# A fused attention and mixture kernel on one core: a new order for its 2,644 steps

## The chip, the cores and the metric

One Trainium2 chip, one of its cores. The metric is the device time of one execution in microseconds (us); lower is better. TensorE is called PE here, VectorE DVE, ScalarE ACT, GpSimd POOL, and SyncE, which issues the DMAs, SP.

## The reference

Attention with a learned bias over positions, followed by a soft mixture of experts. Sizes: 8 batches, 8 heads, 576 positions, head size 64; 8 experts with 4 slots each, inner size 1024; all in float32.

```python
scores = q @ k.T / sqrt(D)
x = log1p(abs(i - j)) / log1p(max(i, 1))
h = maximum(x[..., None] @ w1 + b1, 0)
scores += (h @ w2).transpose(2, 0, 1)
attn = softmax(scores)
x = (attn @ v).reshape(8 * 576, 512)
logits = x @ phi
slot_input = softmax(logits, axis=0).T @ x
slot_out[e] = maximum(slot_input[e] @ moe_w1[e], 0) @ moe_w2[e]
return softmax(logits, axis=1) @ slot_out
```

## The kernel before

**Stages.** First the bias tables are made (36 jobs): for each job ACT or DVE writes four feature rows (steps `f`, lines 975 and 977), PE multiplies them with the bias weights (`B`, line 987), ACT or DVE copies the product out of PSUM (`E`, lines 997 and 995) and SP stores it to a table in DRAM, `bias_m` (`D`, line 1006). From there it is read back, slanted, into tiles `bm` and `br` (`b`, line 425), once for each pair of heads.

Then come 40 units of attention (a pair of heads of one batch; for the first pair each batch is two smaller units, so units 0 to 15 are pair 0 and units 16 to 39 are pairs 1 to 3). A unit has two to four tiles of 128 query rows, and every second one also a fifth, numbered 4, made of the last 64 rows of two units. Tile p of unit u goes through these steps: scores on PE (`S`), bias and row minimum on DVE (`t`, line 534, twice, one a head), exponential on ACT (`e`, line 542, twice), 1e-9 added to the row sums on DVE or POOL (`a`, line 549), reciprocal on DVE (`m`, line 553), scaling on POOL (`n`, line 436, twice), transposes on PE (`T`, and `R` for the last 64 columns, line 495), copies into `at` on ACT or DVE (`c`, `cR`, line 439). The products with v are three steps `M0`, `M1`, `M2` of a unit (PE, line 629), whose result `x` copies and `xs` stores. `lq` and `lv` load q, k and v of a unit (lines 413 and 418).

In the units of the last pair, 32 to 39, the mixture joins in: `fx` reads a batch's stored results back (line 654, tile `xo`), `K`, `KR` transpose them, `L` makes logits (line 709), `D`, `W`, `C`, `Z` the running softmax and slot sums. Expert weights (`w`, `r`, line 957 and, for two tiles, 955; 64 of them, 512 KB each) are fetched as buffers fall free. At the end come the experts (`F`, line 1074; `s`, line 1147), `k` (transposes of the combine weights, lines 1120 and 1123), `g` (line 1157) and the outputs: products `o` (line 1179) and `X`, copies `p`, stores `P` (line 1187).

**Two forms of a score tile.** Line 509: `S` of tiles 0 to 3 is made either as two products of 64 rows by 128 columns of the PE array (line 517), here called *halves*, or as four of 64 by 64 (line 523), called *quarters*. The trace shows 8 matmul records of a tile in halves and 16 in quarters, since float32 takes two passes. Fifth tiles are always in quarters. Products with v use 64 by 64, transposes 64 by 128.

**What sets the order.** A table, `ORDER` (lines 24 to 245): each entry names a step and its unit, then a `+` that selects the other engine for a copy (for `S`: quarters), then after `@` the PSUM banks (eight banks; a tile of two banks starts at 0, 2, 4 or 6). The steps are sorted by their place in it, with no scheduler behind it (lines 481 to 488 and 1220):

```python
        def run():
            given[:] = spots
            f(eng)

        prog.append((at, len(prog), run))
...
        for _, _, f in sorted(prog, key=lambda x: x[:2]):
            f()
```

Each engine, SP's DMA issues included, works through its own instructions in this order and waits where an input is not there or a buffer is not free.

Of the kernel before, what the change touches and what calls it, by code (L numbers as in the profile page):

```python
# [29 lines left out]
f21.3/-1+ E8/-1 E10/-1 f16.1/-1+ f18.2/-1+ D14/-1 D12/-1 E19/-1 f16.3/-1 f17.0/-1 f23.1/-1+ f21.1/-1  # L30
B21/-1@6 f22.1/-1 f22.0/-1 f16.0/-1 B16/-1@4 f18.1/-1 f18.0/-1 B18/-1@2 E21/-1 f20.2/-1 D13/-1 D8/-1
f23.2/-1 f23.0/-1 f23.3/-1 B23/-1@0 D10/-1 E16/-1 D21/-1 f22.2/-1+ f22.3/-1 B22/-1@6 f1.2/-1 f17.3/-1
f17.2/-1 f17.1/-1+ B17/-1@4 f1.1/-1 E18/-1+ f20.0/-1+ f20.1/-1+ f5.0/-1 f3.1/-1+ E23/-1+ f0.2/-1 D19/-1
E22/-1 b1/-1 D16/-1 B20/-1@2 E20/-1+ E17/-1 D18/-1 f3.0/-1 f3.3/-1+ f1.0/-1+ S1/0@6,0 f5.1/-1
D22/-1 D23/-1 t1.0/0 S1/1+@4,2 t1.0/1 f1.3/-1+ B1/-1@6 f0.3/-1 t1.1/0 f5.2/-1 f3.2/-1+ B3/-1@4
f0.1/-1 f5.3/-1+ e1.0/0 e1.1/0 t1.1/1 f2.0/-1 D17/-1 B5/-1@0 a1/0 m1/0 E5/-1+ f0.0/-1+
f4.2/-1 B0/-1@2 E0/-1+ E1/-1 f2.3/-1+ f2.1/-1 f4.0/-1 S2/0@6,0 E3/-1 f2.2/-1+ f4.1/-1 D20/-1
b2/-1 f4.3/-1 e1.1/1 t2.1/0 lq/2 t2.0/0 n1.0/0 n1.1/0 T1/0@4 c1/0 B2/-1@2 E2/-1
B4/-1@4 E4/-1+ e2.1/0 S2/1@0,2 lq/3 e2.0/0 a2/0+ m2/0 e1.0/1 n2.1/0 t2.0/1 t2.1/1
a1/1+ S1/2@6,4 t1.1/2 f7.3/-1+ e2.0/1 n2.0/0 D0/-1 e2.1/1 a2/1 f7.2/-1 t1.0/2 m2/1  # L40
T2/0@0 c2/0 S2/2@2,4 f7.0/-1 m1/1 t2.1/2 e1.0/2 f30.3/-1 f27.3/-1 R2/0@6 t2.0/2 cR2/0
D5/-1 f6.1/-1 f7.1/-1 M0/0@0 f6.2/-1+ M1/0 lq/4 n2.0/1 f26.3/-1+ M2/0 lv/2 x/0
xs/0 e1.1/2 D4/-1 f6.0/-1 n2.1/1 T2/1@4 c2/1 n1.0/1 n1.1/1 T1/1@6 f24.1/-1 c1/1
R2/1@2 e2.1/2 cR2/1+ f27.0/-1 D2/-1 f28.2/-1 B7/-1@0 E7/-1+ D7/-1 a1/2 m1/2 n1.0/2
n1.1/2 f26.0/-1 S1/3+@2,4 t1.1/3 t1.0/3 e2.0/2 a2/2 e1.1/3 m2/2 f31.1/-1 f32.2/-1 M0/1@6
M1/1 S2/3+@0,4 t2.0/3 t2.1/3 f28.0/-1+ f26.1/-1 f24.2/-1 e1.0/3 D3/-1 D1/-1 a1/3+ m1/3
M2/1 x/1 f6.3/-1+ f33.0/-1 f26.2/-1 T1/2@2 c1/2 n2.1/2 n2.0/2 R2/2@0 f27.2/-1 T2/2@6
B6/-1@4 f33.3/-1 cR2/2 c2/2 f30.1/-1 E6/-1 S1/4+@2,0 t1.1/4 t1.0/4 M0/2@6 M1/2 n1.1/3
n1.0/3 f27.1/-1+ S2/4+@4,0 f25.2/-1+ M2/2 f28.3/-1 lq/5 B26/-1@2 t2.0/4 x/2+ e2.1/3 f28.1/-1+
e2.0/3 e1.0/4 e1.1/4 a1/4 t2.1/4 e2.1/4 f24.0/-1 B27/-1@4 f24.3/-1 E27/-1 a2/3 f33.1/-1  # L50
f30.0/-1 lq/6 m2/3 n2.0/3 B24/-1@6 E24/-1 E26/-1+ n2.1/3 D6/-1 D26/-1 m1/4 B28/-1@0
E28/-1+ n1.0/4 e2.0/4 a2/4+ T1/3@4 R2/3@2 c1/3+ cR2/3 xs/1 T2/3@6 lv/4 f25.1/-1
m2/4 n2.0/4 S1/5@0,2 D28/-1 t1.0/5 t1.1/5 n1.1/4 c2/3 D27/-1 S2/5@4,6 t2.1/5 t2.0/5
f34.0/-1 f30.2/-1+ B30/-1@0 f31.0/-1+ f32.1/-1+ n2.1/4 E30/-1 T1/4@2 c1/4+ f25.0/-1 R2/4@6 cR2/4
T2/4@4 e2.0/5 c2/4 S1/6+@0,6 t1.1/6 lv/3 M0/3@2 f32.0/-1 M0/4@4 f31.2/-1 M1/3 M1/4
M2/3 f29.3/-1 f29.0/-1 xs/2 D30/-1 f32.3/-1 f29.1/-1+ t1.0/6 f34.2/-1 M2/4 x/4+ b0/-1
f35.1/-1 lq/7 e1.1/5 e1.0/5 a1/5+ m1/5 n1.0/5 D24/-1 S2/6+@6,0 t2.1/6 t2.0/6 f25.3/-1+
x/3 B25/-1@2 f31.3/-1+ f29.2/-1+ xs/3 f34.3/-1+ e2.1/5 a2/5 f35.0/-1 lq/8 lv/5 m2/5
n2.0/5 e1.0/6 f35.3/-1+ B29/-1@4 E25/-1+ E29/-1+ B31/-1@0 E31/-1 B32/-1@6 n2.1/5 T2/5@2 E32/-1+
e1.1/6 c2/5+ lv/6 n1.1/5 R2/5@4 D25/-1 cR2/5 T1/5@0 c1/5 D29/-1 D31/-1 a1/6+  # L60
f35.2/-1 S1/7@6,4 t1.1/7 D32/-1 t1.0/7 S0/8@2,0 t0.0/8 b3/-1 m1/6 n1.0/6 f34.1/-1+ B34/-1@4
E34/-1+ D34/-1 B35/-1@6 E35/-1+ D35/-1 e2.1/6 e2.0/6 a2/6+ f33.2/-1+ B33/-1@2 m2/6 n2.1/6
e1.0/7 e1.1/7 a1/7+ m1/7 t0.1/8 n1.0/7 E33/-1 e0.0/8 S2/7+@4,6 D33/-1 t2.0/7 e2.0/7
M0/5@2 M1/5 lq/9 t2.1/7 e2.1/7 a2/7+ xs/4 m2/7 n1.1/7 S3/8+@0,4 t3.0/8 n2.0/6
M2/5 x/5 lv/7 b4/-1 n1.1/6 t3.1/8 n2.1/7 T1/6@6 c1/6 n2.0/7 R2/6@0 cR2/6+
T1/7@2 c1/7 xs/5 R2/7@4 T2/7@0 cR2/7+ c2/7+ T2/6@6 c2/6 S0/9+@4,2 t0.0/9 t0.1/9
S4/8@0,6 e0.1/8 a0/8 M0/6@4 M0/7@2 M1/6 M1/7 lq/10 e3.1/8 e3.0/8 a3/8+ m3/8
n3.0/8 n3.1/8 M2/6 t4.0/8 e4.0/8 t4.1/8 e4.1/8 x/6+ xs/6 m0/8 M2/7 x/7+
a4/8 n0.0/8 e0.0/9 m4/8 n4.0/8 S3/9+@0,6 t3.1/9 e0.1/9 e3.1/9 t3.0/9 S0/10@4,2 t0.1/10
T3/8@6 c3/8 n0.1/8 t0.0/10 T0/8@0 c0/8 R3/8@2 cR3/8+ n4.1/8 R4/8@4 T4/8@6 c4/8  # L70
cR4/8+ a0/9 m0/9 n0.0/9 S3/10@2,4 t3.1/10 e3.0/9 lv/9 e0.1/10 e3.1/10 t3.0/10 a3/9+
m3/9 n0.1/9 lv/8 M0/8@0 lq/11 S4/10@6,4 t4.0/10 e4.0/10 n3.1/9 n3.0/9 t4.1/10 e4.1/10
a4/10 m4/10 n4.0/10 n4.1/10 M1/8 M2/8 x/8 R3/9@2 cR3/9 xs/7 T3/9@6 T0/9@4
c0/9 c3/9+ S0/11+@0,2 t0.0/11 e3.0/10 a3/10 e0.0/11 m3/10 n3.0/10 S3/11+@6,4 t3.0/11 t3.1/11
lq/12 M0/9@0 M1/9 w0/22 lv/10 t0.1/11 lq/13 n3.1/10 e0.0/10 a0/10+ m0/10 n0.0/10
b0/15 S0/12+@6,4 t0.0/12 e3.0/11 M2/9 lv/11 n0.1/10 e3.1/11 e0.1/11 t0.1/12 a0/11 m0/11
n0.0/11 R4/10@2 cR4/10+ x/9 T4/10@6 c4/10+ T0/10@0 c0/10 a3/11 S3/12@4,2 R3/10@6 m3/11
# [1200 lines left out]
```

## Time and profile before

| what | value |
|---|---|
| median of 3 runs | 575.78 us (574.41 to 576.62) |
| the profiled execution's own time | 573.29 us |
| its span in the trace | 571.5 us |
| PE busy | 538.3 us, 94% |
| DVE busy | 432.6 us, 76% |
| ACT busy | 434.1 us, 76% |
| POOL busy | 238.7 us, 42% |
| DMA | 117.13 MB, 205 GB/s on average |

Busy time is the union of an engine's instructions; the rest of the span the engine stood still. Matmuls overlap, four at a time in quarters, so the distance from one step's start to the next step's start tells more of PE than the duration of one record. The span leaves out 1.8 us of the execution's own time.

### The profile page before, as it was taken

Reading aid. Unit: us, or ns where it says so; the run is one execution under the profiler, and the core shown is the slowest. Engines: PE = TensorE matmul, PEld = TensorE weight load, DVE = VectorE, ACT = ScalarE, POOL = GpSimd, SP = SyncE. Lnnn points to the kernel's source line nnn. Section 1 sums busy time; section 2 is a strip of 40 time slices with the busy share of each in tenths; the row PEclk is TensorE's granted clock in tenths of the full one; section 3 lists DMA queues with packets and bytes.
Section 4 is the critical chain, followed back from the end, with each engine's and each line's share of the span. In section 5 each row is a group of like instructions: output and inputs, shape, how many; then the busy total and the mean of one; then the engine's idle time right before and its main releaser. Section 6 shows DMA issues by size and latency. Waiting matters only on the chain.

```text
span 571.5 us, 23414 instructions
## 1 busy us (share of the span) xinstructions
PE 538.3 (94%) x9847; PEld 374.3 (65%) x9847; DVE 432.6 (76%) x1186; ACT 434.1 (76%) x913; POOL 238.7 (42%) x376
## 2 busy tenths in 40 slices
...
GB/s 182 225 202 254 122 256 327 219 227 268 243 123 159 103 225 103 117 309 24 287 80 180 74 64 209 127 313 67 155 108 221 142 24 235 368 380 380 406 359 332
DMA packets 46552, 117.13 MB, mean 205 GB/s; under 512 B 5488, under 2 KB 9712, under 8 KB 46448
## 3 DMA queue, kind: packets, MB, share of 16 engines
...
q8 instruction: 77, 1.26, 0.9%
q10 hardware_dynamic: 144, 0.29, 0.1%
q14 instruction: 27, 0.22, 0.1%
...
## 4 chain that ended last, share of the span: by engine, by line
PE 72%; DVE 10%; DMA 6%; ACT 5%; issue 3%; POOL 3%; DVEq 0%; POOLq 0%; SPq 0%; ACTq 0%
PE ps L629 20%; PE ps L523 15%; PE ps L495 14%; PE ps L517 6%; PE ps L987 4%; DVE y L534 4%; DVE f L977 3%; POOL y L436 3%; PE ps L1147 3%; DMA xo<-xs 3%; PE ps L1074 2%; DMA v<-in_v_dram 2%; ACT y L542 2%; PE ps L709 2%; DMA qk<-in_qk_dram 1%
## 5 line engine op out<-in xcount | busy, mean ns | idle before, releaser
L436 POOL TENSOR_SCALAR y<-y,sm 128x576 f32<-128x576 f32 x288 | 213.0, 755 | 165.8 <-DVE sm L553 131.4
L542 ACT ACTIVATE y<-y,mn 128x576 f32<-128x576 f32 x288 | 220.6, 769 | 23.2 <-DVE mn L534 20.2
L534 DVE CUSTOM_DVE_ANT_0 y<-ps,bm 128x576 f32<-128x576 f32 x256 | 185.0, 752 | 49.8 <-PE ps L523 33.4
L629 PE MATMUL ps<-at,v 64*64 64x288 f32 (+2 forms) x2880 | 162.6, 357 | 1.7 <-DMA v<-in_v_dram 1.1
L439 ACT COPY at<-ps 128x1024 f32<-128x1024 f32 (+2 forms) x139 | 110.2, 808 | 29.4 <-PE ps L495 26.2
L523 PE MATMUL ps<-qk 64*64 64x512 f32 (+1 forms) x1552 | 119.7, 408 | 5.6 <-DMA qk<-in_qk_dram 2.4
L629 PEld LDWEIGHTS ps<-at,v 64*64 64x64 f32 x2880 | 103.8, 133 | 24.8 <-ACT at L439 1.2
L495 PE MATMUL ps<-ident,y 64*128 64x64 f32 x2592 | 106.7, 227 | 6.5 <-DVE mn L534 2.7
L495 PEld LDWEIGHTS ps<-ident,y 64*128 64x128 f32 x2592 | 93.7, 139 | 25.4 <-POOL y L436 11.3
L523 PEld LDWEIGHTS ps<-qk 64*64 64x64 f32 x1552 | 71.2, 133 | 58.5 <-issue 37.4
L439 DVE COPY at<-ps 128x256 f32<-128x256 f32 (+2 forms) x85 | 72.4, 858 | 8.0 <-PE ps L495 6.4
L517 PE MATMUL ps<-qk 64*128 64x512 f32 (+1 forms) x376 | 61.6, 436 | 0.2 <-DVE at L439 0.2
L542 ACT ACTIVATION_READ_ACCUMULATOR y<-y,mn 128x1 f32 x288 | 54.8, 190 | 0.0
L517 PEld LDWEIGHTS ps<-qk 64*128 64x128 f32 x376 | 42.3, 187 | 17.5 <-issue 12.5
L549 POOL TENSOR_SCALAR sm<-sm 128x2 f32<-128x2 f32 x67 | 15.0, 225 | 83.8 <-ACT y L542 78.8
L977 DVE TENSOR_SCALAR f<-tabs,scl,nb 128x400 f32<-128x400 f32 (+17 forms) x95 | 44.5, 523 | 1.6 <-ACT e L997 1.2
L987 PE MATMUL ps<-f,wbd 128*32 128x79 f32 (+48 forms) x640 | 41.4, 390 | 3.1 <-DVE f L977 2.4
L975 ACT ACTIVATE f<-tabs,cols,scl 128x368 f32<-128x368 f32 (+17 forms) x49 | 34.3, 748 | 3.2 <-DVE scl L341 1.8
L987 PEld LDWEIGHTS ps<-f,wbd 128*32 128x32 f32 x640 | 20.3, 110 | 22.4 <-issue 11.1
L553 DVE RECIPROCAL sm<-sm 128x2 f32<-128x2 f32 x144 | 22.9, 162 | 13.5 <-POOL sm L549 11.0
L534 DVE CUSTOM_DVE_ANT_0 y<-ps,br 128x576 f32<-128x576 f32 x32 | 23.2, 753 | 8.4 <-PE ps L523 7.5
L439 ACT COPY xts<-ps 128x576 f32<-128x576 f32 (+2 forms) x27 | 14.9, 550 | 15.2 <-PE ps L629 13.9
...
## 6 DMA issues: line engine op xcount, KB each, us to landing
...
```

Of the source, the lines that this page charges most:

```text
L436: nc.gpsimd.tensor_scalar(out=out, in0=y, scalar1=r, scalar2=1.0, op0=ALU.mult, op1=ALU.mult)
L439: (nc.vector.tensor_copy if eng else nc.scalar.copy)(out=out, in_=in_)
L495: nc.tensor.matmul(out, src[rs], ident[rs, rs], is_transpose=True, start=True, stop=True, tile_position=(64 * r, 0))
L517: nc.tensor.matmul(pss[hh].t[:, n, 0:w], x[rs, S + QP[p]:S + QP[p] + P], x[rs, ks], start=True, stop=True, tile_position=(64 * hh, 0))
L523: nc.tensor.matmul(pss[hh].t[64 * r:64 * r + 64, n, 0:w], x[rs, q0:q0 + 64], x[rs, ks], start=True, stop=True, tile_position=(64 * hh, 64 ...
L534: nc.vector.tensor_tensor_reduce(out=d["y", p][:, :, hh], in0=blocks(d["ps", p][hh].read().rearrange("a n j -> a (n j)")[:, 0:S]), in1=blo ...
L542: nc.scalar.activation(out=y, in_=y, func=AF.Exp, bias=d["mn", p][:, hh:hh + 1], scale=-1.0, accum_out=d["sm", p][:, hh:hh + 1])
L553: nc.vector.reciprocal(out=r, in_=r)
L629: nc.tensor.matmul(d["po"].t[64 * c:64 * c + 64, hh, 0:n], d["v"][rs, 64 * k:64 * k + 64], at[0][rs, k, c, cs], start=k == 0, stop=k == 8, ...
L975: nc.scalar.activation(out=f, in_=tabs[:, 0:n], func=AF.Relu, bias=cols[:, 1:2], scale=sc)
L977: nc.vector.tensor_scalar(out=f, in0=tabs[:, 0:n], scalar1=sc, scalar2=nb1[:, 0:1], op0=ALU.mult, op1=ALU.max)
L987: nc.tensor.matmul(pb.t[32 * t:32 * t + 32, a // 512, a % 512:a % 512 + c1 - c0], wbd, x, start=True, stop=True, tile_position=(0, 32 * t))
```

## The change

Only the table `ORDER` is replaced. It has the same 2,644 steps. Different are their order, the `+` marks and the bank numbers. Counted from the two tables: 115 score tiles in quarters where there were 97 (halves 29, were 47); of the 144 copies `c` DVE does 58 (48), of the 80 `cR` 41 (37), of the 144 sums `a` 88 (77), of the 40 `x` 8 (13), of the 36 `E` 10 (15). All 23 weight tiles that take over the buffers of the bias stage are fetched before the last unit; two of them stood in the last stage before. The first lines of the table:

```diff
 ORDER = """
-f12.0/-1+ f11.1/-1+ f12.3/-1 f15.0/-1 f13.2/-1+ wm/-1 f9.0/-1+ f9.2/-1+ f13.0/-1+ f12.1/-1 f12.2/-1 B12/-1@0
+wm/-1 f13.2/-1+ f13.0/-1+ f14.2/-1 f9.1/-1 f13.3/-1+ f15.3/-1+ f15.0/-1 f15.1/-1+ f13.1/-1 f14.0/-1 B13/-1@0
```

PE from the last third of unit 21's products to the first of unit 22's. `ident,y` are transposes (an entry x16 is one tile), `at,v` products, `128x512` a score tile in halves, `64x512` one in quarters. Before:

```order
L629 MATMUL ps<-at,v 64x288 x12
L495 MATMUL ps<-ident,y 128x64 x18
L517 MATMUL ps<-qk 128x512 x2
L517 MATMUL ps<-qk 128x64 x2
L495 MATMUL ps<-ident,y 128x64 x20
L517 MATMUL ps<-qk 128x512 x2
L517 MATMUL ps<-qk 128x64 x2
L495 MATMUL ps<-ident,y 128x64 x48
L517 MATMUL ps<-qk 128x512 x2
L517 MATMUL ps<-qk 128x64 x2
L495 MATMUL ps<-ident,y 128x64 x4
L629 MATMUL ps<-at,v 64x288 x12
```

With the change:

```order
L629 MATMUL ps<-at,v 64x288 x12
L495 MATMUL ps<-ident,y 128x64 x38
L517 MATMUL ps<-qk 128x512 x2
L517 MATMUL ps<-qk 128x64 x2
L523 MATMUL ps<-qk 64x512 x4
L523 MATMUL ps<-qk 64x64 x4
L495 MATMUL ps<-ident,y 128x64 x48
L523 MATMUL ps<-qk 64x512 x4
L523 MATMUL ps<-qk 64x64 x4
L495 MATMUL ps<-ident,y 128x64 x4
L629 MATMUL ps<-at,v 64x288 x12
```

Two of the three score tiles between transposes have gone from halves to quarters, and the transposes of two tiles now stand together.

SP where q and k of unit 9 are loaded (`qk`), before:

```order
L425 DMA bm<-bias_m 128x2x576
L1006 DMA bias_m<-e 128x591 x6
L413 DMA qk<-in_qk_dram 128x1152
L641 DMA xs<-xts 256x1x128
L418 DMA v<-in_v_dram 128x576
L425 DMA br<-bias_m 128x2x576
```

With the change:

```order
L425 DMA bm<-bias_m 128x2x576
L1006 DMA bias_m<-e 128x591 x4
L413 DMA qk<-in_qk_dram 128x1152
L418 DMA v<-in_v_dram 128x576 x2
L641 DMA xs<-xts 256x1x128
L425 DMA br<-bias_m 128x2x576
```

Four stores of the bias table stand between the last `bm` load and `qk`, not six, and two loads of v, not one, go ahead of the store `xs` and of `br`.

PE at the end, from the second experts' products (`wt,hT`) to the first outputs (`cT,ss`), before:

```order
L1147 MATMUL ps<-wt,hT 32x128 x96
L1157 MATMUL ps<-so,small 128x128
L1120 MATMUL ps<-ident,ck 128x128 x4
L1123 MATMUL ps<-ident,ck 32x64 x4
L1157 MATMUL ps<-so,small 128x128
L1179 MATMUL ps<-cT,ss 128x512 x8
```

With the change:

```order
L1147 MATMUL ps<-wt,hT 32x128 x96
L1157 MATMUL ps<-so,small 128x128
L1120 MATMUL ps<-ident,ck 128x128 x4
L1123 MATMUL ps<-ident,ck 32x64 x4
L1179 MATMUL ps<-cT,ss 128x512 x8
L1157 MATMUL ps<-so,small 128x128
```

The second `g` (line 1157) stands behind the first outputs, no longer ahead of them.

## Rows read from the trace of the kernel before

**Rows 1.** The page's first part: busy time of each engine.

```profile
PE 538.3 (94%) x9847; PEld 374.3 (65%) x9847; DVE 432.6 (76%) x1186; ACT 434.1 (76%) x913; POOL 238.7 (42%) x376
```

**Rows 2.** Busy time by stretch: start:end, length, engines in turn, PE clock, DMA share, GB/s.

```profile
200.00:250.00 50.00, 48.89 (x827) 34.30 (x829) 37.05 (x105) 41.90 (x91) 28.37 (x45) 1.00 0.52 177
...
540.00:545.00 5.00, 3.51 (x50) 1.86 (x52) 2.54 (x4) 2.21 (x4) 0.00 (x0) 1.00 0.80 318
545.00:550.00 5.00, 5.00 (x136) 4.12 (x128) 1.26 (x3) 1.48 (x4) 0.00 (x0) 1.00 1.00 390
```

**Rows 3.** Timeline of PE, units 20 and 21: start, length, what.

```profile
208.93 1.30 PE L517 MATMUL ps<-qk 64*128 64x512 f32 x8
210.06 1.93 PE L495 MATMUL ps<-ident,y 64*128 64x64 f32 x48
211.92 1.20 PE L523 MATMUL ps<-qk 64*64 64x512 f32 x16
213.05 0.34 PE L495 MATMUL ps<-ident,y 64*128 64x64 f32 x4
...
214.83 1.15 PE L523 MATMUL ps<-qk 64*64 64x512 f32 x16
215.80 1.64 PE L629 MATMUL ps<-at,v 64*64 64x288 f32 x24
217.26 1.15 PE L523 MATMUL ps<-qk 64*64 64x512 f32 x16
218.23 1.64 PE L629 MATMUL ps<-at,v 64*64 64x288 f32 x24
219.80 1.33 PE L495 MATMUL ps<-ident,y 64*128 64x64 f32 x36
```

**Rows 4.** The chain that ended last, around the load of unit 9's q and k.

```profile
92.59 1.14 PE ps L523 x16
...
95.80 6.27 DMA qk<-in_qk_dram
```

**Rows 5.** Timeline of PE and of SP there; in brackets the idle time before.

```profile
102.20 2.06 PE L523 MATMUL ps<-qk 64*64 64x512 f32 x24 [2.36 <-DMA qk<-in_qk_dram]
...
91.48 4.22 SPq L1006 DMA_DIRECT2D bias_m<-e  x6
```

**Rows 6.** The chain that ended last, two loads of stored results.

```profile
473.89 7.25 DMA xo<-xs
...
497.85 7.13 DMA xo<-xs
```

**Rows 7.** Who PE waited for: total us, times, longest.

```profile
PE ps L629 <- DMA v<-in_v_dram: 1.1, 2, 0.9
PE ps L709 <- DMA xo<-xs: 1.1, 1, 1.1
...
PE ps L495 <- DMA xo<-xs: 0.5, 1, 0.5
```

**Rows 8.** Timeline of DVE, the copy that the first bias product waits for.

```profile
6.69 0.16 DVE L377 COPY bcon<-ps 128x4 f32<-128x4 f32 x1 [0.62 <-PE ps L375]
```

**Rows 9.** Timeline from the last `k` to the first store of the output.

```profile
539.36 0.60 PE L1120 MATMUL ps<-ident,ck 128*128 128x128 f32 x4
...
541.35 0.31 PE L1123 MATMUL ps<-ident,ck 64*32 64x64 f32 x6 [1.16 <-issue]
...
542.01 2.00 PE L1179 MATMUL ps<-cT,ss 32*128 32x512 f32 x16
...
544.30 2.88 SPq L1187 DMA_DIRECT2D out_dram<-ob  x4
```

**Rows 10.** Time from issue to landing of the loads of v (line 418).

```profile
DMA to landing us min/median/max: 2.7/4.8/7.7
```

**Rows 11.** The same for the bias tiles `br`.

```profile
DMA to landing us min/median/max: 3.7/4.7/6.1
```

**Rows 12.** Groups of instructions by shape: count, busy us, mean ns, idle before, releaser.

```profile
L439 DVE COPY at<-ps 128x1024 f32<-128x1024 f32 x48 | 58.5, 1219 | 5.2 <-PE ps L495 3.9 <-ACT xk L439 0.4 <-ACT lp L439 0.3
```

More of the change, by code (lines that the diff above doesn't have):

```diff
@@ L30 @@
[L30 to L77, printed above, removed]
@@ new lines @@
+f0.3/-1 D20/-1 S1/0@0,4 t1.1/0 t1.0/0 e1.0/0 e1.1/0 S1/1+@2,6 t1.1/1 t1.0/1 D22/-1 b2/-1
+f3.3/-1 B5/-1@4 f1.0/-1+ f1.1/-1 E5/-1 B0/-1@0 E0/-1 S2/0@6,2 e1.1/1 lq/2 f1.3/-1 e1.0/1
+a1/0 m1/0 f1.2/-1 B1/-1@4 f3.0/-1 f3.2/-1 E1/-1 f4.3/-1 D1/-1 B3/-1@0 f2.3/-1 n1.0/0
+n1.1/0 T1/0@4 E3/-1 f6.3/-1+ f2.2/-1 a1/1 D3/-1 f2.0/-1 f2.1/-1 c1/0 f4.1/-1 B2/-1@0
+E2/-1 f4.0/-1 f4.2/-1 t2.1/0 e2.1/0 t2.0/0 e2.0/0 f6.1/-1+ f27.1/-1+ B4/-1@4 E4/-1+ D2/-1
+a2/0+ m2/0 n2.1/0 n2.0/0 S2/1+@2,0 lq/3 m1/1 t2.0/1 e2.0/1 t2.1/1 S1/2+@6,4 t1.1/2
@@ new lines @@
+t1.0/2 e2.1/1 a2/1+ m2/1 T2/0@2 c2/0 f7.1/-1 S2/2@0,4 t2.1/2 t2.0/2 f24.0/-1 R2/0@6
+M0/0@2 f7.3/-1 D0/-1 f25.2/-1+ cR2/0 n1.1/1 f24.1/-1+ n1.0/1 T1/1@6 c1/1 n2.1/1 n2.0/1
+T2/1@4 R2/1@0 cR2/1+ e2.1/2 f7.2/-1 c2/1+ f7.0/-1 M1/0 e2.0/2 f24.2/-1+ S1/3+@6,0 t1.1/3
+M2/0 f26.1/-1 f6.2/-1 x/0 xs/0 M0/1@4 a2/2 m2/2 e1.1/2 B7/-1@2 M1/1 lq/4
+t1.0/3 f35.3/-1 e1.1/3 e1.0/2 a1/2+ m1/2 f27.3/-1 lv/2 S2/3+@0,6 f6.0/-1 t2.0/3 f26.0/-1+
+E7/-1 M2/1 t2.1/3 D7/-1 f27.0/-1+ f27.2/-1 x/1 xs/1 e1.0/3 n2.1/2 n2.0/2 lv/3
@@ new lines @@
+lq/5 n1.0/2 n1.1/2 T2/2@2 T1/2@0 R2/2@4 c1/2 cR2/2+ f28.2/-1+ c2/2+ f30.1/-1 B6/-1@6
+D5/-1 E6/-1 e2.1/3 f26.2/-1 D6/-1 f28.3/-1+ a1/3 m1/3 n1.0/3 S1/4+@4,0 t1.1/4 t1.0/4
+f26.3/-1+ f28.0/-1 f28.1/-1 M0/2@2 M1/2 e2.0/3 a2/3 f24.3/-1 S2/4+@6,0 lq/6 t2.0/4 e1.0/4
+M2/2 x/2+ lv/4 m2/3 n2.1/3 t2.1/4 xs/2 e1.1/4 n2.0/3 e2.0/4 e2.1/4 a2/4
+B28/-1@4 a1/4+ m1/4 f29.2/-1 E28/-1+ D4/-1 f30.3/-1 B26/-1@6 E26/-1 B27/-1@2 f30.2/-1 f30.0/-1+
+n1.1/3 B24/-1@0 R2/3@6 E27/-1 D27/-1 m2/4 cR2/3+ T1/3@4 c1/3+ f29.1/-1 E24/-1 T2/3@2
@@ new lines @@
+c2/3 S1/5@6,0 n2.0/4 f34.2/-1+ n1.1/4 t1.1/5 e1.1/5 n1.0/4 S2/5@4,2 n2.1/4 t1.0/5 e1.0/5
+t2.0/5 t2.1/5 B30/-1@0 E30/-1 T1/4@6 c1/4 b0/-1 f32.2/-1 R2/4@4 a1/5+ m1/5 T2/4@2
+c2/4 cR2/4+ f31.0/-1 f32.3/-1 f31.1/-1 f31.2/-1 D24/-1 f32.0/-1 M0/3@0 S1/6+@4,6 t1.0/6 f35.2/-1
+t1.1/6 D28/-1 D30/-1 M0/4@2 M1/3 M1/4 e2.1/5 D26/-1 M2/3 b2/15 lv/5 f31.3/-1
+e2.0/5 lq/7 f29.3/-1 M2/4 x/4+ f33.3/-1 f35.1/-1 a2/5 S2/6+@4,6 m2/5 f25.0/-1+ t2.0/6
+f29.0/-1+ B29/-1@2 xs/4 E29/-1+ x/3 xs/3 f25.1/-1+ f33.0/-1+ f25.3/-1+ B25/-1@0 e1.0/6 lq/8
@@ new lines @@
+e1.1/6 D29/-1 n1.1/5 n2.1/5 E25/-1 B31/-1@4 f32.1/-1 E31/-1 f34.3/-1 D31/-1 f35.0/-1 B32/-1@2
+E32/-1 D25/-1 D32/-1 t2.1/6 e2.1/6 n2.0/5 f34.0/-1 T2/5@0 a1/6+ m1/6 c2/5+ n1.0/5
+R2/5@4 cR2/5+ f34.1/-1+ B35/-1@6 E35/-1 T1/5@2 c1/5+ f33.2/-1+ n1.1/6 f33.1/-1+ S1/7@0,4 t1.1/7
+B34/-1@6 E34/-1+ D35/-1 b3/-1 D34/-1 t1.0/7 e2.0/6 e1.1/7 B33/-1@2 E33/-1 D33/-1 e1.0/7
+a2/6+ m2/6 n2.1/6 S0/8+@4,6 S2/7+@0,2 t0.1/8 e0.1/8 lq/9 t0.0/8 e0.0/8 a1/7 m1/7
+n1.0/6 t2.1/7 n2.0/6 n1.0/7 e2.1/7 n1.1/7 t2.0/7 M0/5@6 T1/6@4 c1/6+ e2.0/7 a2/7+
@@ new lines @@
+m2/7 M1/5 S3/8+@2,0 t3.0/8 t3.1/8 M2/5 x/5 lv/6 lv/7 T2/6@4 R2/6@2 cR2/6+
+T1/7@6 c1/7+ xs/5 b4/-1 n2.1/7 c2/6 n2.0/7 a0/8+ m0/8 n0.1/8 R2/7@0 T2/7@2
+cR2/7 S0/9+@4,0 c2/7 t0.1/9 e0.1/9 S4/8@6,2 lq/10 t0.0/9 e0.0/9 t4.1/8 M0/6@0 e3.1/8
+e3.0/8 a3/8+ m3/8 M0/7@4 n3.1/8 M1/7 M2/7 x/7 e4.1/8 n3.0/8 t4.0/8 n0.0/8
+M1/6 lv/9 S3/9+@2,4 t3.1/9 lq/11 e4.0/8 a4/8+ m4/8 n4.0/8 n4.1/8 M2/6 lv/8
+x/6 xs/6 t3.0/9 e3.1/9 R3/8@6 cR3/8+ S0/10@4,0 t0.0/10 T3/8@2 c3/8 t0.1/10 T4/8@6
+c4/8+ T0/8@4 c0/8 S3/10+@0,2 t3.1/10 e3.0/9 a3/9 m3/9 n3.0/9 e0.0/10 w1/21 n3.1/9
@@ new lines @@
+a0/9+ m0/9 n0.1/9 n0.0/9 M0/8@6 xs/7 R4/8@4 cR4/8+ M1/8 S4/10@2,4 lq/12 M2/8
+t3.0/10 e0.1/10 e3.0/10 t4.1/10 T3/9@0 t4.0/10 c3/9+ e3.1/10 a3/10+ x/8 m3/10 n3.0/10
+R3/9@4 cR3/9 T0/9@6 c0/9 a0/10+ m0/10 n0.0/10 n3.1/10 S0/11+@2,4 t0.1/11 t0.0/11 S3/11+@0,6
+lq/13 t3.0/11 n0.1/10 e4.1/10 e4.0/10 a4/10 m4/10 t3.1/11 n4.0/10 e0.0/11 e0.1/11 a0/11+
+m0/11 M0/9@4 lv/10 e3.0/11 M1/9 S0/12+@2,0 t0.1/12 e3.1/11 t0.0/12 M2/9 x/9 T0/10@6
+n4.1/10 c0/10 n0.0/11 lv/11 R4/10@0 cR4/10+ T4/10@4 c4/10 a3/11 m3/11 n3.0/11 n3.1/11
```

349 lines of the change are left out of this document (177 added, 172 removed).

## The prediction

> **What bounds the kernel now.** I read the busy times first: PE is busy for 94% of the span, the next engines for 76% [rows 1]. Then the stretches: in the middle of the attention PE is busy 48.89 of 50 us, DVE 37.05 and ACT 41.90, and the DMA engines half the time [rows 2]. PE sets the pace there, and it hardly stands still; what an order can still win lies in how tightly its steps follow each other, and that is read from the starts of steps in its timeline [rows 3]. Last I read the chain of waits and the list of who waited for whom, for the places where PE does stand still: loads of q and k [rows 4, 5], loads of stored results [rows 6, 7], the start [rows 8] and the end [rows 9]. From the first store of the output, at 544.3, the DMA engines are full (share 1.00) [rows 2, 9], so the last 27 us only move with that first store.
>
> A difference of under 0.5% (2.9 us) can't be told from no change in a measurement of this kernel.
>
> **The change, part by part.** All steps stay, so PE's work changes in one way only: 18 score tiles go from halves to quarters. Counts below are from the order, times from the rows.
>
> *Forms of the score tiles.* A tile in quarters with products around it takes 0.97 us from start to start (214.83 to 215.80; 217.26 to 218.23), one in halves between transposes 1.13 (208.93 to 210.06) [rows 3]. That would be 18 x 0.16 = 2.9 us gained. But a tile in quarters between transposes takes 1.13 as well (211.92 to 213.05) [rows 3]: there nothing is won. Tiles of this kind are 16 in the new order and 2 in the old, so 14 of the 18 give 0, and 4 give 4 x 0.16 = 0.6 us. A change of form costs also elsewhere: a third of a unit's products takes 1.46 us when a score tile in quarters follows (215.80 to 217.26) and 1.57 when transposes follow (218.23 to 219.80) [rows 3], 0.11 more. In PE's order the form changes between 64x64 and 64x128 121 times, 76 before; 28 of the 45 more lie around the 14 tiles already priced, and 17 x 0.11 = 1.9 us remain. Together **+1.3 us**. Bounds: -1.9 if the changes lie in time that PE waits anyway (0.6 for the four tiles, and 14 x 0.09 if the transposes that follow start no later than after halves, which no row excludes); +4.3 if each of the 45 costs 0.16 and all 18 tiles earn 0.16 back. I take the value nearest to the rows of the same neighbourhood.
>
> The Trainium skill, page "TensorEngine Tiling (Array Packing)", section "Tiling Modes", says that a change of the tiling mode, not just of the tile, drains TensorE. By it all 45 changes would be paid, which is the upper bound, +4.3, and not the +1.3 taken. The trace agrees that a change costs (0.11 and 0.16), not that the tile in halves is the cheaper one beside it.
>
> *q and k of unit 9.* Before, the load is issued at 95.80, behind six stores of the bias table that SP issued from 91.48 to 95.70, though the score tile that frees its buffer ends at 93.73; it lands after 6.27 us, and PE waits 2.36 us [rows 4, 5]. Now the last of these bias rows is copied before the next exponentials on ACT, no longer after two of them, so SP should be free when the buffer is. The PE work between release and use is as long as before. Issued about 1.9 us earlier, the load leaves a wait of some 0.5: **-1.8 us**; nothing if SP is still late, -2.4 if the load is quicker.
>
> *Stored results of batches 5 to 7.* These loads take 7.25 and 7.13 us [rows 6], and PE waits 0.5 and 1.1 for two of them [rows 7]. The PE work between the last reader of the buffer and the first use of the new data, counted with the lengths that steps have at their quickest, grows from 6.4, 6.4 and 5.3 us to 7.8, 8.4 and 5.9. The first wait goes, the last shrinks by 0.6: **-1.1 us** (0 to -1.6).
>
> *Start.* DVE stands still 0.62 us in front of the copy of the bias offsets, since PE is still in its warm-up products (`wm`) [rows 8]. With the change five feature rows of DVE stand before that copy, not four, and the work is there anyway: **-0.6** (0 to -0.6), in a stage where DVE and ACT are the busy ones.
>
> *End.* Inside the last `k` PE stands still 1.16 us at nothing that the profile shows, and then `g` goes first; the outputs begin 2.65 us after `k` does (539.36 to 542.01) [rows 9]. Now `g` stands behind the first outputs (0.2 to 0.5 us of PE) and the instructions lie elsewhere in PE's stream. I take **-1.2** (0 to -1.7); the DMA share of 0.80 between 540 and 545 shows that the stores can start earlier [rows 2]. The two weight tiles that leave this stage earn nothing more: PE works without a gap there and isn't waiting for weights.
>
> *New waits.* Two loads get less time. Unit 8's v: the PE work from the release of its buffer to its use falls from 4.5 to 3.7 us, while such a load takes 4.8 at the median and 7.7 at most [rows 10]: **+0.8** (0 to +3.2, the part of 7.7 over 4.5). What waits is `M0` of unit 8, with all of PE behind it. The first `br`: on SP it is now behind two loads of v and a store `xs`, which waits for the copy of unit 5's products; from that store to the first use of `br` lie 4.3 us of PE work, 7.4 from the issue before. The load takes 4.7 at the median, 6.1 at most [rows 11], with 0.8 us for the two issues: **+1.2** (0 to +2.6). What waits is a `t` on DVE, and behind it all of DVE's queue and the four banks of that score tile.
>
> *Work moved between DVE, ACT and POOL.* In units 8 to 31 DVE gets four more copies into `at` (4 x 1.22 us [rows 12]), seven more sums and one small copy, and loses four `x`: about 4 us in 275. I cost it at nothing, since DVE is idle for a quarter of that time [rows 2]. If that cover were gone, what is late next are the `t`, whose banks PE needs, and the cost is up to those 4 us.
>
> *The sum:* 1.3 - 1.8 - 1.1 - 0.6 - 1.2 + 0.8 + 1.2 = **-1.4 us**. The profiled execution took 573.29 (span 571.5 and 1.8 around it), 2.5 below the median of 575.78, so it becomes 571.9 there, and 574.4 on the scale of the median. That is my forecast: no change that can be told, a little to the faster side.
>
> **The rivals.**
>
> *Faster: the changes of form are free and the new loads in time.* PE's small gaps before scores and products are waits for copies and banks; a change of form in the same place costs nothing. Then the forms give -1.9, the two new waits 0, and the sum is -1.9 - 1.8 - 1.1 - 0.6 - 1.2 = -6.6: **569.2 us**. For it speaks that the same bank is asked for again too soon in fewer places (less than 0.8 us of PE work after its last use: 66 pairs of banks, 72 before). Against it: PE is busy 98% in the middle, so there is little to hide in [rows 2].
>
> *No change, by another way: every change of form is paid.* +4.3 in place of +1.3 makes the sum +1.6: **577.4 us**. It is what the rule of the Trainium skill quoted above comes to, at 0.16 a change.
>
> *Slower: SP's single queue makes loads late.* SP issues in order; a load that stands behind a waiting store waits too. If v of unit 8 and `br` come at their longest (+3.2 and +2.6) and unit 9's q and k stay as late as before (0 for -1.8), the sum is 1.3 - 1.1 - 0.6 - 1.2 + 3.2 + 2.6 = +4.2: **580.0 us**. It decides from the point where these three loads together cost 4.5 us, 4.3 more than my terms for them have (+0.2). For it: the waits at 102.2 came in just this way [rows 5]. Against: PE's two waits for v came to 1.1 us in all [rows 7], at leads that are hardly longer.
>
> **How the numbers follow.** The forecast has a chance of 0.32, the faster rival 0.36, the paid changes 0.16 (of which 0.06 end over +0.5%, with one of the waits added), the late loads 0.16. So faster by over 0.5% has 0.36, within 0.5% 0.32 + 0.10 = 0.42, slower 0.06 + 0.16 = 0.22. The forecast's own range, with the single terms at their ends one at a time, is 571.2 to 577.4. The whole range goes down to 567.0, 2 us below the faster rival, where the `k` and q/k terms are at their ends and a few bank waits go too, and up to 580.5, just past the late loads.
>
> **What would show it.** In the changed kernel's profile: PE's timeline with tiles in quarters between transposes at about 1.13 us from start to start, and thirds of products at 1.57 before transposes; the load of unit 9's q and k issued within 0.5 us of the end of the score tile that frees it, with PE waiting under 1 us; waits for `xo` of at most 0.6 in sum; no stop in `k` before the first outputs; a wait on `br` of about 1 us on DVE. The forecast is wrong if PE's busy time moves by more than 4 us, if PE's waits for q and k, v and `xo` pass 8 us in sum (2.4 + 1.1 + 1.6 = 5.1 before [rows 5, 7]), or if the DMA share after the first store of the output falls well below 1.00.

## The result, and the profile after

| kernel | median | runs |
|---|---|---|
| before | 575.10 us | 6, 574.13 to 576.62 |
| with the change | 567.37 us | 6, 566.10 to 568.63 |

The ratio is 0.9863, 95% interval 0.9838 to 0.9888: 7.7 us faster. The forecast was 574.4, no change that can be told; the time lies inside the range, but 0.4 us from its lower end and beside the faster rival's 569.2. The profiled execution took 566.71 us, its span is 564.7 where it was 571.5.

Busy time of each engine with the change, then three stretches (start:end, length, PE, PEld, DVE, ACT, POOL, PE clock, DMA share, GB/s):

```profile
PE 537.2 (95%) x9991; PEld 358.6 (64%) x9991; DVE 430.8 (76%) x1188; ACT 435.8 (77%) x922; POOL 232.7 (41%) x365
```

```profile
200.00:250.00 50.00, 49.61 (x872) 34.33 (x868) 39.35 (x114) 43.47 (x94) 28.42 (x44) 1.00 0.42 143
...
540.00:545.00 5.00, 4.67 (x140) 3.81 (x136) 1.08 (x3) 2.67 (x4) 0.00 (x0) 1.00 1.01 394
545.00:550.00 5.00, 4.25 (x54) 2.70 (x58) 2.68 (x5) 2.90 (x5) 0.00 (x0) 1.00 0.94 366
```

Beside [rows 1] PE's busy time fell by 1.1 us only, but the time that PE stands still fell from 33.2 to 27.5. In the 50 us from 200 on PE is busy 49.61, not 48.89 [rows 2].

To see where the lead comes from, I took the start of the same steps in both timelines. `M0` is the first third of a unit's products, `F` the experts' first layer, `o` the first outputs. By each point PE has nearly the same steps behind it in both.

| PE starts (us) | before | change | lead |
|---|---|---|---|
| `M0` of unit 0 | 44.5 | 44.0 | 0.5 |
| `M0` of unit 8 | 114.4 | 109.7 | 4.7 |
| `M0` of unit 16 | 176.0 | 170.9 | 5.1 |
| `M0` of unit 32 | 381.4 | 371.4 | 9.9 |
| `F` | 515.9 | 508.0 | 7.9 |
| `o` | 542.0 | 535.1 | 6.9 |

So 4.7 us come from the stage in which bias tables and first units run together, 4.8 from units 16 to 31, and 3.0 are given back at the end. In units 16 to 31 the sum had next to nothing. There it is PE's waits that went, most of them short. Who PE waited for, from the first products of unit 16 to those of unit 32 (total us, times, longest), before:

```profile
PE ps L523 <- DVE mn L534: 1.4, 4, 0.5
PE ps L629 <- DMA v<-in_v_dram: 1.1, 2, 0.9
PE ps L495 <- POOL y L436: 1.0, 3, 0.4
PE ps L495 <- DVE mn L534: 0.9, 3, 0.4
PE ps L495 <- ACT at L439: 0.4, 1, 0.4
```

and with the change, the whole answer:

```profile
PE ps L495 <- DVE mn L534: 1.3, 4, 0.5
PE ps L523 <- DVE mn L534: 0.3, 1, 0.3
```

"DVE mn" is a `t` that still reads the bank a new score tile or transpose needs, "POOL y" a scaling that a transpose reads, "ACT at" a copy. The list sets out only the clear ones. Counted by the distance from step to step, 13 steps of this stretch take 0.4 us or more longer than their kind does at its quickest, about 7.5 us in all, and 5 with the change, about 2.4 in all. The stretch itself, before and with the change (columns as above):

```profile
176.00:381.40 205.40, 199.73 (x3416) 142.06 (x3420) 159.26 (x452) 172.21 (x368) 111.97 (x173) 1.00 0.46 155
```

```profile
170.90:371.40 200.50, 198.60 (x3494) 135.14 (x3490) 161.48 (x458) 169.59 (x364) 109.37 (x164) 1.00 0.47 157
```

PE's idle time falls from 5.7 to 1.9 us, its busy time by 1.1. Not all of the 4.8 need belong to the order: the two waits for v (1.1 us) are absent from e1 below, which runs this stretch in the order before and takes 204.0 us where the profile of before takes 205.4.

What is lost again later, in PE's timeline with the change (in brackets the idle time before):

```profile
449.51 0.27 PE L495 MATMUL ps<-ident,lq 64*128 64x64 f32 x1 [1.66 <-POOL lq L780]
...
504.16 2.54 PE L860 MATMUL ps<-xk,ek 128*32 128x128 f32 x40
...
517.53 1.09 PE L1096 MATMUL ps<-ident,hS 128*128 128x128 f32 x8 [0.76 <-ACT hS L1088]
...
533.41 0.63 PE L1147 MATMUL ps<-wt,hT 128*32 128x128 f32 x11 [1.58 <-issue]
533.97 0.49 PE L1157 MATMUL ps<-so,small 128*128 128x128 f32 x2
534.30 0.60 PE L1120 MATMUL ps<-ident,ck 128*128 128x128 f32 x4
534.83 0.32 PE L1123 MATMUL ps<-ident,ck 64*32 64x64 f32 x8
535.07 2.00 PE L1179 MATMUL ps<-cT,ss 32*128 32x512 f32 x16
```

Three things stand here. Transposes of the running softmax of batch 3 wait 1.66 us for a small fill on POOL (`lq`, line 780), which stands behind a scaling there. The last slot sums (line 860) take 2.54 us, 1.41 before, because PE is granted the lower of its two clocks for them. And the stop that stood inside the last `k` [rows 9] is gone from there but stands, 1.58 us long, just ahead, in front of the last 11 matmul records of a second expert.

### The profile page after: what moved, and what is told of

It reads as the page before. It is cut to its first block, busy times and chain, and to the rows that moved or that the text cites. A ratio compares the mean times of both kernels' runs of the same rounds, so it can differ in the third digit from the quotient of the medians.

```text
span 564.7 us, 23724 instructions
## 1 busy us (share of the span) xinstructions
PE 537.2 (95%) x9991; PEld 358.6 (64%) x9991; DVE 430.8 (76%) x1188; ACT 435.8 (77%) x922; POOL 232.7 (41%) x365
## 4 chain that ended last, share of the span: by engine, by line
PE 72%; DVE 8%; ACT 5%; DMA 3%; issue 3%; POOL 1%; SPq 1%; ACTq 0%; DVEq 0%; POOLq 0%
PE ps L629 22%; PE ps L523 17%; PE ps L495 17%; PE ps L517 5%; DVE y L534 4%; PE ps L1074 2%; ACT y L542 2%; PE ps L1147 2%; DVE f L977 2%; PE ps L709 1%; DMA out_dram<-ob 1%; PE ps L851 1%; DMA qk<-in_qk_dram 1%; DMA bias_m<-e 1%; ACT ob L439 1%
## 5 line engine op out<-in xcount | busy, mean ns | idle before, releaser
L523 PE MATMUL ps<-qk 64*64 64x512 f32 (+1 forms) x1840 | 139.3, 409 | 0.6 <-DVE mn L534 0.3
L439 ACT COPY at<-ps 128x1024 f32<-128x1024 f32 (+2 forms) x125 | 99.7, 806 | 28.1 <-PE ps L495 23.9
L523 PEld LDWEIGHTS ps<-qk 64*64 64x64 f32 x1840 | 78.5, 132 | 66.2 <-issue 47.8
L629 PEld LDWEIGHTS ps<-at,v 64*64 64x64 f32 x2880 | 99.4, 133 | 27.0 <-issue 1.2
L439 DVE COPY at<-ps 128x1024 f32<-128x1024 f32 (+2 forms) x99 | 85.3, 875 | 7.6 <-PE ps L495 6.7
L977 DVE TENSOR_SCALAR f<-tabs,scl,nb 128x352 f32<-128x352 f32 (+17 forms) x94 | 44.6, 530 | 0.5 <-DMA bias_m<-e 0.4
L987 PE MATMUL ps<-f,wbd 128*32 128x512 f32 (+46 forms) x640 | 41.6, 390 | 2.5 <-DVE f L977 1.7
L517 PE MATMUL ps<-qk 64*128 64x64 f32 (+1 forms) x232 | 37.0, 433 | 0.0
L975 ACT ACTIVATE f<-tabs,cols,scl 128x368 f32<-128x368 f32 (+16 forms) x50 | 34.2, 735 | 2.4 <-DVE scl L341 1.9
L517 PEld LDWEIGHTS ps<-qk 64*128 64x128 f32 x232 | 22.3, 188 | 12.9 <-issue 11.3
```

Of the source, the lines that this page charges most:

```text
L439: (nc.vector.tensor_copy if eng else nc.scalar.copy)(out=out, in_=in_)
L517: nc.tensor.matmul(pss[hh].t[:, n, 0:w], x[rs, S + QP[p]:S + QP[p] + P], x[rs, ks], start=True, stop=True, tile_position=(64 * hh, 0))
L523: nc.tensor.matmul(pss[hh].t[64 * r:64 * r + 64, n, 0:w], x[rs, q0:q0 + 64], x[rs, ks], start=True, stop=True, tile_position=(64 * hh, 64 ...
L629: nc.tensor.matmul(d["po"].t[64 * c:64 * c + 64, hh, 0:n], d["v"][rs, 64 * k:64 * k + 64], at[0][rs, k, c, cs], start=k == 0, stop=k == 8, ...
L975: nc.scalar.activation(out=f, in_=tabs[:, 0:n], func=AF.Relu, bias=cols[:, 1:2], scale=sc)
L977: nc.vector.tensor_scalar(out=f, in0=tabs[:, 0:n], scalar1=sc, scalar2=nb1[:, 0:1], op0=ALU.mult, op1=ALU.max)
```

## The experiments

All change only the table. The kernel before was run beside each; a ratio is always to it. Since whole runs scatter by 3 us and more, each is also read by its leads at the steps of the table above. A lead compares one profiled execution with the one of before; those of e1 and e4 are the slowest of their runs, that of e2 the fastest of its four.

| lead in us at | change | again | e1 | e2 | e8 | e3 | e4 | e6 |
|---|---|---|---|---|---|---|---|---|
| `M0` of 8 | 4.7 | 1.7 | 1.7 | 4.1 | 3.5 | 4.8 | -3.2 | -2.5 |
| `M0` of 16 | 5.1 | 2.6 | -0.6 | 5.1 | 4.5 | 5.8 | -2.9 | -5.0 |
| `M0` of 32 | 9.9 | 7.4 | 0.8 | 9.9 | 9.3 | 10.5 | -2.7 | -0.5 |
| `F` | 7.9 | 5.4 | 1.7 | 9.9 | 10.1 | 8.3 | -3.0 | -2.5 |
| `o` | 6.9 | 4.5 | 1.3 | 9.5 | 9.1 | 7.3 | -5.0 | -2.7 |
| gained from 16 to 32 | 4.8 | 4.8 | 1.4 | 4.8 | 4.8 | 4.7 | 0.2 | 4.5 |

### The change once more

Nothing is edited.

> The changed kernel itself once more, beside the others on the same chip: 566 to 569 us, 1.1 to 1.6% faster than before.

567.73 us, ratio 0.9878 (0.9836 to 0.9919). Its profile ("again" above) is worth the run: between the first profile of the change and this one 3.0 us lie at unit 8, and from unit 16 to unit 32 both gain the same 4.8. Most of the scatter arises where the bias tables, their stores and the loads of q and k share the DMA engines; behind the first outputs another 1.4 us arise (29.5 to 30.9 us from `o` to the end in the profiles of the table). From unit 16 to unit 32 the new order repeats itself to 0.1 us in the five profiles that have it from the start (200.6 to 200.7 us). The order before does not: 205.4 us before, 204.0 in e1, 204.5 in e9, 205.2 in e4, in part by how long PE waits for v (1.1, 0, 1.0 and 1.1 us). So the last row of the table decides more than a median, but as a gain over one profile of before, which can be 1.4 us off: the stretch itself is worth 3.4 to 4.8 us.

### e1: the new start alone

```diff
 R4/10@0 cR4/10+ T4/10@4 c4/10
-a3/11 m3/11 n3.0/11 n3.1/11 S3/12+@2,0 t3.0/12
+w0/22 b0/15 a3/11 S3/12@4,2 R3/10@6 m3/11
...
```

Ahead of this place the table is the new one, behind it the one before (what has been done already left out).

> The new order up to its 632nd step (the transposes of unit 10's last tile, at about 121 us), then the rest of the steps in the order before. At this point the changed kernel leads by 4.3 to 5.1 us (first products of units 10 and 9: 126.3 against 131.4, 117.2 against 122.2). Theory A, the gains are made stage by stage in PE's small gaps and add up: 4 to 5.5 us faster than before, about 570.3 us where before takes 575.1. Rival B, a lead is used up later, since loads set when the later steps run: at most 1.5 us faster, 573.6 to 575.1.

570.32 us, ratio 0.9934 (0.9909 to 0.996): 3.8 us faster, near theory A, and B's 1.5 lies outside. The profiled execution is the slowest of the six (572.37); its lead of 1.7 at unit 8 is as in the second profile of the change, and 2.3 are lost at the seam up to unit 16. Of the 1.4 gained from 16 to 32, where its order is the one before, 1.1 are the waits for v, which did not come.

### e2: the new order up to unit 34, the old end

```diff
 w0/19 a1/34 K01/32@4 kc01/32+
-S4/34@0,2 t4.1/34 c0/33 e0.1/34
+w0/22 w0/31 w0/17 w1/20 w0/16 w0/25 m1/34 c0/33 S4/34@4,2
...
```

> The new order up to its 1950th step (scores of unit 34's fifth tile, 382.3 us against 392.5), then the order before for the rest, the experts and the outputs included. The lead is 10.2 us there and 6.9 at the first outputs (535.1 against 542.0), so the changed kernel loses 3.3 us of it in units 34 to 39 and the experts. Theory A, each stage keeps what its own order gives: the whole lead of 10 stays, about 565 us against 575.1 before, 2.5 us faster than the changed kernel. Rival B, the lead runs into loads of weights and stored results that come no earlier, whatever the order: 567 to 568.5, no faster than the changed kernel.

565.69 us, ratio 0.9848 (0.9824 to 0.9873). By the median 8.6 us were gained, between A and B and not to be told from the change alone. The leads speak for A: 1.1 us are lost at the seam and won back in the old end (9.9 at unit 32, 9.9 at `F`, 9.5 at `o`), where the new end gives back 3.0.

### e8: the same, cut later

```diff
 M0/34@4 e2.0/35 D/33@2 a2/35
-n3.0/35 t1.1/36 n3.1/35 dq/33+
+w0/22 w0/17 w1/20 w0/25 t1.1/36 n3.1/35 m2/35 dq/33+
...
```

> As the new order up to unit 34 with the order before behind it, but cut 111 steps later, ahead of the scalings of unit 35's last tile. The lead at that point is 10.0 to 10.5 us (slot sums of batch 1: 413.6 against 424.2; first products of unit 35: 421.8 against 431.8), and the earlier cut lost 1.1 at its seam. Theory A, the lead stays and this seam costs less: 0.5 to 1 us below the earlier cut, 564.5 to 565.3, and 2 to 3 us faster than the changed kernel. Rival: this seam costs as much or more, 565.5 to 567.4, not to be told from the changed kernel.

565.12 us, ratio 0.9831 (0.9789 to 0.9873). Against the change once more, run beside it, the means of six lie 2.6 us apart (95% interval 0.8 to 4.4). It beats both kernels: the lead of 9.3 at unit 32 is 10.1 at `F`. In both profiles of the change 2.0 us are lost between these points.

### e3 and e4: the forms of the score tiles

e3 is the changed kernel with the forms of the kernel before, e4 the kernel before with the new forms; 26 marks each.

```diff
-S1/29+@0,4
+S1/29@0,4
...
```

> The changed kernel with the forms of the score tiles of the kernel before: 22 tiles back from quarters to halves, 4 from halves to quarters. Three prices. Forms as predicted (+1.3 us for the new ones): 1.3 us faster than the changed kernel, 566.1. Every change of form paid (+4.3): 563.1. Changes of form free and a tile in quarters 0.13 us quicker: 18 x 0.13 = 2.3 us slower, 569.7.

> The kernel before with the forms of the score tiles of the changed kernel, the order, banks and engines as before: 22 tiles from halves to quarters, 4 back. As predicted (+1.3 us): 576.4 where before takes 575.1. Every change of form paid: 579.4. Changes of form free: 2.3 us faster, 572.8.

e3: 566.61 us, ratio 0.9866 (0.984 to 0.9892), the changed kernel's own 0.9863. e4: 577.59 us, 1.0059 (1.0034 to 1.0083), 3.4 us slower. By the medians the forms cost between nothing and 3.4. The leads speak against these 3.4 as a price of the tiles: from unit 16 to 32, where 9 of the 18 more tiles in quarters lie, e4 gains 0.2 and e3 loses 0.1 to the change; from unit 32 to `F` e4 loses 0.2. Its loss arises by unit 8 (3.2), ahead of which four tiles differ, and between `F` and `o` (2.0), beside loads and the stops described in the last section. How much of it every execution has, one profile, the slowest of eight, can't tell. In the new order, where this stretch repeats to 0.1 us, the forms are worth about 0.1 in 200; in the order before, where it scatters by 1.4, e4's 0.2 says no more than that they are under that.

### e6: the new middle alone

```diff
 T4/10@6 c4/10+ T0/10@0 c0/10
-a3/11 S3/12@4,2 R3/10@6 m3/11
+b2/15 w1/21 a3/11 m3/11 n3.0/11 n3.1/11 S3/12+@2,0
...
```

and back to the order before at `S4` of unit 34.

> The order before up to its 632nd step (about 126 us), then the new order up to the scores of unit 34's fifth tile, then the order before again. In this stretch the changed kernel's lead grows by 4.8 us in units 16 to 31 (from 5.1 to 9.9). Theory A, this gain is the stretch's own: 4 to 5 us faster than before. Rival B, it needs the earlier start, since loads in the middle come at times of their own: at most 1.5 us faster.

575.84 us, ratio 1.0031 (1.0005 to 1.0057): no gain, as B has it. But B's reason isn't in the profile. 2.5 us are behind at unit 8, ahead of any edit, which is the scatter of that stage; 2.5 more go by unit 16, at the first seam, 1.1 at the second; from unit 16 to 32 this kernel gains 4.5 (200.9 us). Who PE waited for there is the list of the changed kernel again:

```profile
PE ps L495 <- DVE mn L534: 1.3, 4, 0.5
PE ps L523 <- DVE mn L534: 0.3, 1, 0.3
PE ps L495 <- ACT at L439: 0.2, 1, 0.2
```

The gain of the stretch is its own and needs no early start. What one can't do is cut a stretch out for nothing: four of the five seams of e1, e2, e6 and e8 cost 1 to 2.5 us, e8's none that shows.

### e9: unit 9's load alone

```diff
-a2/6+ f33.2/-1+ B33/-1@2 m2/6 n2.1/6 e1.0/7 e1.1/7 a1/7+ m1/7 t0.1/8 n1.0/7 E33/-1 e0.0/8 S2/7+@4,6 D33/-1
+a2/6+ f33.2/-1+ B33/-1@2 m2/6 n2.1/6 E33/-1 D33/-1 e1.0/7 e1.1/7 a1/7+ m1/7 t0.1/8 n1.0/7 e0.0/8 S2/7+@4,6
```

> The kernel before with two steps moved: the copy and the store of the last bias row of this group (E33, D33) stand ahead of the exponentials of unit 7's tile 1 instead of behind them and the reciprocal, so that SP reaches the load of unit 9's q and k earlier. As predicted: the load goes out about 1.9 us earlier and PE's wait at 102.2 falls from 2.4 to 0.5 us, 1.8 us faster in all. Rival: the load takes longer among the other transfers and the wait stays over 1.5 us, or the two exponentials that are now later delay a product, and nothing is gained.

572.97 us, ratio 0.9988 (0.997 to 1.0006): nothing that can be told. SP and PE in its profile:

```profile
92.09 4.21 SPq L1006 DMA_DIRECT2D bias_m<-e  x6
96.40 1.25 SPq L413 DMA_DIRECT2D qk<-in_qk_dram  x1
```

```profile
96.66 1.32 PE L523 MATMUL ps<-qk 64*64 64x512 f32 x10 [1.00 <-DVE mn L534]
...
108.59 1.36 PE L629 MATMUL ps<-at,v 64*64 64x128 f32 x41 [0.84 <-issue]
```

The last row is ready earlier and the load goes out no earlier (96.40, with this execution 0.6 late all along): SP issues six stores in a row, 0.7 us each, and that run of stores, not the copy at its end, holds the load. PE's wait for q and k is gone all the same, since PE comes later: it now waits 1.00 us for a `t` and 0.84 at a stop of the kind told of in the last section. The result is the rival's; whether the two exponentials that were put off delay that `t` was not followed.

### e5, e7 and e12: which engine does the copies

e5 is the kernel before with the new marks on all steps but `S` (278), e7 the changed kernel with the old ones, e12 the changed kernel with the old marks on the copies into `at` alone (78).

```diff
-R3/26@2 cR3/26 m2/27 n2.0/27
+R3/26@2 cR3/26+ m2/27 n2.0/27
...
```

> The kernel before, its order, banks and forms, with the marks for the engine of the changed kernel on all other steps (278 marks differ: 77 sums a, 78 copies c and cR, 61 feature rows f and others). Theory A, the order of the steps is what gains and the choice of engines alone does little: within 2 us of before. Rival B, the choice of engines is what gains: 4 us faster or more. Theory C, order and engines fit each other, so that a mixture loses: 3 us slower or more.

> The changed kernel, its order, banks and forms, with the marks for the engine of the kernel before on all other steps. Theory A, order is what gains: within 2 us of the changed kernel, 565.5 to 569.5. Rival B, engines are what gains: 4 us slower than it or more, 571.5 or above, as before. Theory C, order and engines fit each other: 3 us slower than it or more, and the mixture the other way round (old order, new engines) slower than before too.

> The changed kernel with the engine marks of the kernel before on the copies into at alone (c and cR, 78 of 224 differ; DVE does 85 of them instead of 99). With all 278 marks it was 79 us slower. Theory A, the copies carry most of that, since a copy of 1.2 us put behind other work on the wrong engine holds two banks and a product: 30 us slower or more. Rival B, the copies are free to go to either engine, and the marks of the feature rows and sums did the harm: within 5 us of the changed kernel.

e5: 651.73 us, ratio 1.1362 (1.1322 to 1.1402). e7: 646.91, 1.1274 (1.1247 to 1.1302). e12: 591.40, 1.0297 (1.0258 to 1.0337), 24 us above the change. Theory C, and by far more than its 3 us. The copying engines' busy times hardly differ from e7 to the change, PE's does:

```profile
PE 569.0 (88%) x9991; PEld 365.0 (57%) x9991; DVE 432.0 (67%) x1186; ACT 434.1 (67%) x913; POOL 236.7 (37%) x376
```

Of the 79 us 32 are busy time of PE (537.2 with the change). Part of them is the clock: ahead of the last 7 us PE was granted 0.50 in nine stretches of e7, 44 us in all, which by an estimate from this length can account for 22 us at most (half of it, were PE busy throughout); e5 has 44 us too, e12 7, e10 none. Who PE waited for in e7, units 16 to 31, the four largest:

```profile
PE ps L495 <- POOL y L436: 8.8, 7, 2.6
PE ps L495 <- DVE at L439: 1.9, 2, 1.2
PE ps L523 <- ACT at L439: 1.7, 2, 1.3
PE ps L517 <- DVE xts L439: 1.5, 2, 1.3
```

And DVE's waits over the whole span, in e7 and then with the change:

```profile
DVE at L439 <- PE ps L495: 23.2, 28, 3.6
DVE sm L553 <- POOL sm L549: 18.6, 19, 2.9
```

```profile
DVE at L439 <- PE ps L495: 6.7, 17, 0.7
DVE sm L553 <- POOL sm L549: 5.6, 11, 0.9
```

Reciprocals wait three times as long for sums that now stand in POOL's queue, scalings come later by that, and copies come up on DVE while their product is not there yet. How much work DVE, ACT and POOL have tells nothing here; behind what a step stands does. e12 fell between its theories: the copies alone cost 24 of the 79 us; the rest comes only with the other 200 marks, and whether these alone would cost it was not tried.

### e10: banks by a rule

```diff
-T0/25@4 T3/25@0 c0/25 c3/25 R1/25@2 cR1/25+ S4/26@6,4
+T0/25 T3/25 c0/25 c3/25 R1/25 cR1/25+ S4/26
...
```

> The changed kernel without its bank numbers: each tile takes the bank or pair of banks that has been free longest in the program's order, which gives another place to 428 of 537 steps. Theory A, the order gains and the places add little: within 2 us of the changed kernel. Rival B, the places keep products from waiting for banks: 3 us slower than it or more, 570.5 or above.

597.26 us, ratio 1.0404 (1.0359 to 1.0449): 30 us above the change, rival B tenfold. The same 50 us as in the section on the result:

```profile
200.00:250.00 50.00, 48.58 (x800) 30.27 (x800) 36.33 (x105) 40.65 (x86) 23.87 (x36) 1.00 0.37 119
```

PE is busy 48.58 us, 97%, and does 800 matmuls where the changed kernel does 872; units 16 to 31 take 213.7 us, at a clock of 1.00, with 207.9 of them busy, where the change has 198.6 for the same steps. So the busy share hides a lost pace. DVE's waits for score tiles (line 523) grow from 33.6 us to 47.9 over the span. The rule knows the order of the table only, not when a reader is done; how the waits arise one by one was not followed.

## Why the prediction went as it did

**What bounds.** Right: PE does, at 1.00 of its clock, and an order wins by how tightly PE's steps follow each other. What failed is the sentence against the faster rival, "PE is busy 98% in the middle, so there is little to hide in". What is left over in units 16 to 31 is 5.7 us of idle time, and the change takes 3.8 of them, and 1.1 of the busy time. The sum held named steps only; none of its terms stood for these waits. That the time still lies in the range is luck: the range was let down to 567.0 for other terms, q and k and the `k`, with "a few bank waits" beside them, and the forecast itself is 7 us off.

**Forms, +1.3.** About 0 by the leads of e3; the medians alone do not exclude +1.3. The single prices were right: in units 16 to 31, with the change, a tile in quarters between transposes takes 1.13 us at the median (4 tiles), a third ahead of transposes 1.57 (17). The mistake was to charge 17 changes at 0.11 and to credit 4 tiles: as far as e3's leads tell, what a tile in quarters saves and what the change of form costs come out even. The upper bound of 4.3, a price of 0.16 for every change, is excluded by e3: 4.3 us less than the change would be a ratio of 0.979, and its interval begins at 0.984. The Trainium skill's "TensorEngine Tiling (Array Packing)", section "Tiling Modes", says that each change of the mode drains TensorE, and gives no price; e3 excludes only that one.

**q and k of unit 9, -1.8.** In the first profile it looks right, in the second not:

```profile
87.69 2.60 SPq L1006 DMA_DIRECT2D bias_m<-e  x4
90.39 0.89 SPq L413 DMA_DIRECT2D qk<-in_qk_dram  x1
```

```profile
97.28 1.09 PE L523 MATMUL ps<-qk 64*64 64x512 f32 x8 [0.25 <-DMA qk<-in_qk_dram]
```

```profile
99.34 2.38 PE L523 MATMUL ps<-qk 64*64 64x512 f32 x20 [2.12 <-DMA qk<-in_qk_dram]
```

The load goes out 0.5 us after the score tile that frees its buffer (the two tiles from 87.73 end at 89.93), as foretold. PE then waited 0.25 us in one execution, 2.12 in the other (last row), 0.8 to 1.4 in e2, e3 and e8, and not at all in e1. So the term is -0.2 to -2.4, and the reason given for it (the row copied earlier) is refuted by e9; what is different is that four stores stand there and not six.

**Stored results, -1.1.** No wait for `xo` is left: -1.6, its lower end.

**Start, -0.6.** DVE's stop ahead of the offsets' copy is gone, as said; at the first products of unit 0 it shows as 0.5 in one execution and as nothing in the other.

**End, -1.2.** It came out as +0.9: from `F` to `o` 26.2 us became 27.1. The stop in `k` moved, it did not go, and a wait of 0.76 for ACT came in front. The gain is not there; that the new end is slower in these steps is not shown, since the old end takes 26.2 to 28.2 us in e1, e2, e4, e6, e8 and e9. What the new end does lose, in both profiles, are the 2.0 us from unit 32 to `F`, where the sum had little but the stored results.

**New waits, +0.8 and +1.2.** PE waits for no v any more. DVE waits 1.19 us for the first `br`, the size foretold.

**Work moved between engines, 0.** DVE's and ACT's busy times moved by 1.8 and 1.7 us, and nothing in the change's profile speaks against the 0. But the reason given, the idle time of DVE, does not carry it: e7 has the same busy time on DVE and loses 79 us. Marks are free only together with the order that they belong to.

Of the rivals, the faster one has the right size for partly wrong reasons: the changes of form are free, as it has it, but earn about 0.1 us and not its 1.9; its new waits hold on PE, its q and k and end do not, and of the 4.8 us of units 16 to 31 its terms have only what it says of the forms. The 4.7 us up to unit 8 differ from execution to execution by 3, but are no accident: six profiles with the new start (change, again, e1, e2, e3, e8) reach `M0` of unit 8 at 109.6 to 112.8 us, the four with the old one (before, e4, e6, e9; in e4 and e9 with a few edits) at 114.4 to 117.6. PE stands still for 7.9 to 9.3 us up to there, where it was 11.5 to 14.3: bias products wait 1.0 to 2.0 us for feature rows of DVE, not 2.4 to 3.0, transposes 0.8 for a `t`, not 1.4 or 1.5, and a wait for a sum (0.7) is gone, while those for scalings grow from 0.5 to between 1.0 and 1.7; the stops told of in the last section are shorter, and the wait for q and k is in most. Which moved steps do it was not tried; the one part tried alone (e9) gave nothing.
